# A fused top-k attention and MLP kernel: six MLP chunks of 128 tokens instead of two, no hurried units, kept units further back

## The chip, the cores and the metric

The kernel runs on one core of a Trainium2 chip. The metric is device time in microseconds, from the start to the end of one execution; the median of several runs is given. A core has five engines that work side by side: TensorE (PE in the profile; its weight loads are listed apart as PEld), VectorE (DVE), ScalarE (ACT), GpSimd (POOL) and SyncE (SP), which issues the DMAs. Each engine takes its instructions in the order of the program and waits on semaphores for the others. What follows is about when TensorE is kept from working.

## The reference

Attention over 8 batches of 8 heads, 576 tokens and 64 columns a head, in which each query keeps only its 32 highest scores; then an MLP with a leaky ReLU over the 4608 tokens of all batches, 512 columns wide, 2048 hidden.

```python
scores = scale * np.matmul(q, k.transpose(0, 1, 3, 2))
kth = np.partition(scores, -top_k, axis=-1)[..., -top_k:-top_k + 1]
scores = np.where(scores >= kth, scores, -1000000000.0)
scores = scores - np.max(scores, axis=-1, keepdims=True)
attn = np.exp(scores)
attn = attn / (np.sum(attn, axis=-1, keepdims=True) + 1e-09)
attn_out = np.matmul(attn, v)
...
x = attn_out.transpose(0, 2, 1, 3).reshape(B * S, H * D)
h = x @ w_in
out = np.maximum(0.01 * h, h) @ w_out
```

## The kernel before

**Units and steps.** Attention is cut into 144 units. A unit is 128 query rows of a pair of heads (or twice 64 rows, for what is left of 576), so 32 tokens of all eight heads are worth one unit on average: four units make 128 tokens of x ready, eight make 256. The loop at the end of the program walks through steps `s`; in step `s` unit `s` goes through `top_k` on VectorE (L289: maxima of eight, four rounds), unit `s-1` through mask (GpSimd) and exponents (ScalarE), unit `s-2` through normalising and transposing. Even steps issue the scores of the pair of units `s+2` and `s+3` on TensorE (`scores`, L225).

**Transposing.** The weights of a unit must be transposed before they can be multiplied with the values. `transpose` (L332) has ScalarE split the 32-bit words into halves of 16 bits (L339), writes the halves to DRAM (`apart`, L340) and reads them back with a transposing DMA (L344) into `wT`. `transpose_in_haste` (L346) does the same with nine TensorE transposes (L354), and `keep_transposed` copies the result from PSUM (L360). Units in `HASTY` go that way.

**When values are weighed.** `values_at(n)` gives the step and the place in it, in which unit `n` is multiplied with its values (L381). For `n < 14` that is four steps after the odd unit of the pair, in the middle of the step; from then on three steps after, at its end, and one step sooner for the pairs in `HURRIED`. The result is copied by ScalarE into `x` (L395), of which `xpool` has two buffers.

**The MLP.** `CHUNKS` cuts the 4608 tokens; a chunk is put on the list `ready` when all its units have been weighed. `mlp(ch)` is a generator: it issues matmuls and yields their cost in columns. A chunk of 256 tokens computes hidden values with the weights stationary and x moving (L437, `ph`), 256 columns at a time, then leaky ReLU (L443) into `gT`, then the output (L449, `pz`) with 512 columns. The first `EARLY` chunks, of 128 tokens, take `hidden_of_few` (L399): x is stationary and 512 columns of w_in move (L405), ScalarE applies leaky ReLU into `scale` (L410), and TensorE turns the result in groups of four 128 x 128 transposes (`turned`, L421), which ScalarE copies to `gT` (L422). `ph`, `pt` and `pz` take turns in two PSUM buffers with the tag "ml".

**What sets the order.** Nothing is scheduled by the compiler: the loop calls `mlp_steps(budget)` seven times in a step, which advances the generator until the budget in columns is spent. `slot_budget` gives that budget: as long as no more than the early chunks have become ready it is `EARLY_SHARE`, and later the backlog spread over the slots until the next chunk is ready.

```python
after = [at for (at, _), _ in ready_at if at >= s]
until = after[0] if after else s
if len(after) >= len(CHUNKS) - EARLY:
    return EARLY_SHARE
return backlog[0] / ((until + 1 - s) * SLOTS)
```

**Kept units.** In steps 0 to 5, before any MLP work exists, TensorE computes the scores of twelve units ahead of time (`keep_scores`, L276), from inputs loaded by `load_early`; they are written to DRAM and fetched by `fetch_scores` (L287, 576 KB) three steps before the unit's turn. For `a` in `KEPT` these are units a, a+1, a+8 and a+9. The pairs concerned are then left out when scores are issued.

**SP's queue** carries, in program order, the halves of `split`, the transposing DMAs, the fetches of kept scores, the outputs (L459), and the loads of q, k and v (L651, L179).

Of the kernel before, what the change touches and what calls it, by code (L numbers as in the profile page):

```python
# [20 lines left out]
def kernel(  # L21
# [29 lines left out]
    WCH = 1024  # L51
    LEFT = S % P
    assert D == 64 and S == 576 and HP == 4 and B % 2 == 0 and LEFT == 64
    CHUNKS = [128] * 2 + [256] * 17
    assert sum(CHUNKS) == B * S
    CHMAX = max(CHUNKS)
    LOADED, LOADED_V = 5, 5
# [250 lines left out]
    def mask(u, i):  # L308
        if i == 0:
            u.nbias = small.tile([P, 2], F32, name="nbias")  # L310
            u.z = small.tile([P, 2], F32, name="z")
            nc.gpsimd.tensor_scalar(u.nbias, u.tops[:, :, 0, 0], -SCALE, None, ALU.mult)
        pen = work.tile([P, S], F32, name="pen", bufs=1)
        nc.gpsimd.tensor_scalar(pen, u.s[i], u.tops[:, i, ROUNDS - 1, 7:8], MASKED, ALU.is_lt, ALU.mult)  # L314
        nc.gpsimd.tensor_tensor(u.s[i], u.s[i], pen, ALU.add)  # L315
# [30 lines left out]
    def transpose_in_haste(u):  # L346

        both = u.both.rearrange("p i n -> p (i n)")
        u.parts_T = []
        for c0, c1 in ((0, 8), (8, 2 * NKC - 1)):  # L350
            pt = ps_sc.tile([P, 2, 512], F32, name="wide", bufs=2)
            pt = pt.rearrange("p h (c n) -> p (h c) n", n=P)
            for c in range(c0, c1):
                nc.tensor.transpose(pt[:, c - c0, :], both[:, c * P:(c + 1) * P], ident)  # L354
            u.parts_T.append((c0, c1, pt))

    def keep_transposed(u):
        u.wT = work.tile([P, 2 * NKC - 1, P], F32, name="wT", bufs=3)
        for c0, c1, pt in u.parts_T:
            nc.scalar.copy(u.wT[:, c0:c1, :], pt[:, 0:c1 - c0, :])  # L360

    x_of = {}

    def x_at(token):

        c = 0
        while token >= CHUNKS[c]:
            token -= CHUNKS[c]  # L370
            c += 1
        return c, token
# [15 lines left out]
    def keep_values(u, po):  # L388
        n = u.rows
        po = po.rearrange("p (o n) -> p o n", n=n)  # L390
        ch, col = x_at(u.b * S + u.q0)
        if ch not in x_of:
            x_of[ch] = [xpool.tile([P, CHMAX], F32, name=f"x{c}") for c in range(HP)]
        for o, (pi, _, _) in enumerate(u.outs):
            nc.scalar.copy(x_of[ch][pi % HP][:, col:col + n], po[:, o, :])  # L395

    EARLY = 2

    def hidden_of_few(ch, x):  # L399

        g_of = {}
        for j in range(NFC // 4):
            ph = ps_ml.tile([P, 512], F32, name="ph", tag="ml")
            for c in range(HP):
                nc.tensor.matmul(ph, x[c][:, 0:P], w_in[c][:, j * 512:(j + 1) * 512],  # L405
                                 start=(c == 0), stop=(c == HP - 1))
                if c == 1:
                    yield 2 * 512
            g_of[j] = raws.tile([P, 2 * DMODEL], U16, name="scale", bufs=2).bitcast(F32)
            nc.scalar.activation(g_of[j], ph, AF.Prelu, alpha=SLOPE)  # L410
            yield 2 * 512
            if j:
                yield from turned(j - 1, g_of)
        few[ch] = g_of
# [3 lines left out]
    def turned(j, g_of):  # L418
        pt = ps_ml.tile([P, 4, P], F32, name="pt", tag="ml")
        for i in range(4):  # L420
            nc.tensor.transpose(pt[:, i, :], g_of[j][:, i * P:(i + 1) * P], ident)  # L421
        nc.scalar.copy(gT[:, 4 * j:4 * (j + 1), 0:P], pt)  # L422
        yield 2 * P

    def mlp(ch):

        n = CHUNKS[ch]
        t0 = sum(CHUNKS[:ch])
        x = x_of[ch]
        if ch < EARLY:  # L430
            yield from hidden_of_few(ch, x)
        for f0 in range(0, NFC if ch >= EARLY else 0, 2):
            ph = ps_ml.tile([P, 2, CHMAX], F32, name="ph", tag="ml")
            for i in range(2):
                f = f0 + i
                for c in range(HP):
                    nc.tensor.matmul(  # L437
                        ph[:, i, 0:n], w_in[c][:, f * P:(f + 1) * P], x[c][:, 0:n],
                        start=(c == 0), stop=(c == HP - 1),
                    )  # L440
                    if c == 1 or i == 0 and c == HP - 1:
                        yield 2 * max(n, 225)
            nc.scalar.activation(gT[:, f0:f0 + 2, 0:n], ph[:, :, 0:n], AF.Prelu, alpha=SLOPE)  # L443
            yield 2 * max(n, 225)
        for r0 in range(0, n, P):
            m = min(P, n - r0)
            pz = ps_ml.tile([P, 512], F32, name="pz", tag="ml")
            for f in range(NFC):
                nc.tensor.matmul(  # L449
                    pz[0:m, 0:DMODEL], gT[:, f, r0:r0 + m], w_out[f // 4][:, f % 4, :],  # L450
                    start=(f == 0), stop=(f == NFC - 1),
                )
                if f % 2 and f + 1 < NFC:
                    yield 2 * DMODEL
                if f == 7 and ch in few:
                    yield from turned(NFC // 4 - 1, few[ch])
            o_sb = work.tile([P, DMODEL], F32, name="o_sb", bufs=1)
            nc.scalar.copy(o_sb[0:m], pz[0:m, 0:DMODEL])  # L458
            nc.sync.dma_start(out[t0 + r0:t0 + r0 + m, :], o_sb[0:m])  # L459
            yield 2 * DMODEL  # L460

    def mlp_cost(ch):
        n = CHUNKS[ch]
        if ch < EARLY:
            return NFC * DMODEL + NFC // 4 * (HP * 512 + 2 * P)
# [5 lines left out]
    def mlp_steps(budget):  # L471
        owed[0] += budget
        while owed[0] > 0:
            if running[0] is None:
                if not ready:
                    owed[0] = 0.0
                    return
                running[0] = mlp(ready.pop(0))
            cost = next(running[0], None)
            if cost is None:  # L480
                running[0] = None
            else:
                owed[0] -= cost
                backlog[0] -= cost
# [2 lines left out]

    LAG = 3
    HURRY = 20
    HURRIED = (15, 23, 31)  # L490
    HASTY = (14, 15, 23, 31)
    UNHURRIED = 14
    MIDDLE, END = 0, 1

    def values_at(n):

        if n < UNHURRIED:
            return (n | 1) + LAG + 1, MIDDLE
        return (n | 1) + LAG - ((n | 1) in HURRIED), END

    steps = units

    KEPT = (24, 40, 56)
    EARLY_SCORES = {0: 4, 1: 2, 2: 1, 3: 2, 4: 1, 5: 2}

    def unit(n):
# [3 lines left out]
    for n, u in enumerate(steps):  # L510
        ch, _ = x_at(u.b * S + u.q0)
# [11 lines left out]
    def slot_budget(s):  # L523
# [4 lines that stand above are left out]
            return EARLY_SHARE  # L528
        return backlog[0] / ((until + 1 - s) * SLOTS)

    EARLY_SHARE = 500
    SLOTS = 7

    with tc.manual_schedule():
        last = {p: n for n, u in enumerate(steps) for p in u.pairs}

        to_keep = [[steps[n] for n in (a, a + 1, a + 8, a + 9)] for a in KEPT]
        early_units = {u for us in to_keep for u in us}
# [49 lines left out]
        def weights_of(u):  # L588
            reciprocals(u)
            normalize(u, 0)  # L590
            normalize(u, 1)

        def values(*place):
            due = [u for n, u in enumerate(steps) if values_at(n) == place]
            if due:
                po = ps_sc.tile([P, 2, 512], F32, name="wide", bufs=2)[:, 0, 0:2 * P]
                po = po.rearrange("p (u n) -> p u n", u=2)
            else:
                return ()
            for n, u in enumerate(due):  # L600
                weigh_values(u, po[:, n, :])
            return [(u, po[:, n, :]) for n, u in enumerate(due)]

        def keep(weighed, *place):
            for u, po in weighed:
                keep_values(u, po)
            attended(*place)

        for s in range(len(steps) + LAG + 1):
# [9 lines left out]

            at_first = s < HURRY and s - 2 in HURRIED  # L620
            if at_first:
                weights_of(older)
            slot()
            if old:
                mask(old, 0)
                mask(old, 1)
            late = s < HURRY and not {s - 1, s - 2} & set(HURRIED)
            if older and not late and not at_first:
                weights_of(older)
            mlp_steps(budget)  # L630
            weighed = values(s, MIDDLE)
            at_once = s - 2 in HASTY or any(at == (s, MIDDLE) for at, _ in ready_at)
            if at_once:
                keep(weighed, s, MIDDLE)
            slot()
            if older and late:
                weights_of(older)
            if s - 2 in HASTY:
                transpose_in_haste(older)
# [4 lines left out]
            if older:  # L644
                keep_transposed(older) if s - 2 in HASTY else transpose(older, lambda: mlp_steps(budget))
            if not older or s - 2 in HASTY:
                mlp_steps(budget)
# [83 lines left out]
```

## Time and profile before

| | us |
|---|---|
| median of 3 runs | 1463.28 (1463.24 to 1466.4) |
| the profiled execution | 1463.63 |
| span of the profiled execution | 1461.7 |
| first MLP matmul on TensorE | 130.79 |
| values of units 30 and 31 begin | 372.62 |
| last values begin | 1400.19 |
| MLP of the last chunk begins | 1402.52 |

The granted TensorE clock was 0.985 of full speed over the span. Three forms of rows are used below. A line of groups gives line, engine, operation, output and input, and the busy time. A line of a timeline gives start, duration, engine, line of the kernel, operation, and in brackets the idle time ahead of it with what ended it. A line of the chain of waits gives start, duration and the work that stood on the path that ended last.

Four more groups tell what ScalarE and TensorE do for the small chunks and the hasty units:

```profile
L354 PE MATMUL wide<-ident,s_sb 128*128 128x128 f32 x36 | 5.5, 283 | 0.0
L421 PE MATMUL pt<-ident,scale 128*128 128x128 f32 x32 | 5.0, 278 | 0.0
L410 ACT ACTIVATE scale<-ph 128x512 f32<-128x512 f32 x8 | 4.7, 592 | 1.6 <-PE ph L405 1.6
L422 ACT COPY gT<-pt 128x512 f32<-128x512 f32 x8 | 4.7, 590 | 2.1 <-PE pt L421 2.1
```

### The profile page before, as it was taken

Reading aid. Unit: us, or ns where it says so; the run is one execution under the profiler, and the core shown is the slowest. Engines: PE = TensorE matmul, PEld = TensorE weight load, DVE = VectorE, ACT = ScalarE, POOL = GpSimd, SP = SyncE. Lnnn points to the kernel's source line nnn. Section 1 sums busy time; section 2 is a strip of 40 time slices with the busy share of each in tenths; the row PEclk is TensorE's granted clock in tenths of the full one; section 3 lists DMA queues with packets and bytes.
Section 4 is the critical chain, followed back from the end, with each engine's and each line's share of the span. In section 5 each row is a group of like instructions: output and inputs, shape, how many; then the busy total and the mean of one; then the engine's idle time right before and its main releaser. Section 6 shows DMA issues by size and latency. Waiting matters only on the chain.

```text
span 1461.7 us, 24213 instructions
## 1 busy us (share of the span) xinstructions
PE 1405.5 (96%) x8066; PEld 932.9 (64%) x8068; DVE 1320.3 (90%) x3401; ACT 1100.9 (75%) x1984; POOL 1097.8 (75%) x744
## 2 busy tenths in 40 slices
PE   7848999999989999999999999999999999999998
PEld 2425548576757676767676767676766666666674
DVE  7999999999999999999999999999999999999600
ACT  8878878677868777777778787777777777777710
POOL 3288888878888888888888787888887878787700
PEclk9968999999999999999999999999999999999999
DMA  8967543646576666676656655666566665554510
GB/s 320 344 219 225 140 119 101 194 128 181 151 192 179 172 167 188 156 194 169 157 163 170 169 138 141 171 164 166 149 156 171 164 151 143 153 141 130 150 43 14
DMA packets 394989, 239.03 MB, mean 164 GB/s; under 512 B 334576, under 2 KB 336112, under 8 KB 392944
## 3 DMA queue, kind: packets, MB, share of 16 engines
q1 hardware_dynamic: 394864, 237.48, 58.5%
q8 instruction: 63, 1.03, 0.3%
q14 instruction: 62, 0.51, 0.1%
HBM read 55.77 MB, written 99.09 MB: 106 GB/s over the span
## 4 chain that ended last, share of the span: by engine, by line
PE 77%; DVE 13%; ACT 4%; DMA 4%; issue 1%; SPq 0%; POOL 0%; DVEq 0%; ACTq 0%; POOLq 0%
PE pz L449 30%; PE ph L437 29%; PE wide L381 10%; DVE tops L301 5%; PE wide L225 5%; DVE pairs L304 4%; PE narrow L225 3%; DMA apart<-split 2%; ACT split L339 1%; DVE pairs L296 1%; DMA raw<-in_weights_dram 1%; ACT s_sb L318 1%; ACT s_sb L330 1%; DVE w_out L156 1%; DMA wT<-apart 1%
## 5 line engine op out<-in xcount | busy, mean ns | idle before, releaser
L314 POOL TENSOR_SCALAR pen<-s_sb,tops 128x576 f32<-128x576 f32 x288 | 638.3, 2216 | 203.8 <-DVE tops L301 135.6
L301 DVE MAX8 tops<-pairs 128x8 f32<-128x288 f32 (+1 forms) x1152 | 635.9, 591 | 0.0
L449 PE MATMUL pz<-w_out,gT 128*128 128x512 f32 x1152 | 505.1, 595 | 2.4 <-ACT scale L410 2.4
L437 PE MATMUL ph<-x,w_in 128*128 128x256 f32 x2176 | 482.6, 381 | 0.0
L304 DVE MATCH_REPLACE8 pairs<-tops,pairs 128x288 f32<-128x288 f32 (+1 forms) x864 | 460.1, 538 | 0.0
L437 PEld LDWEIGHTS ph<-x,w_in 128*128 128x128 f32 x2176 | 409.5, 190 | 75.5 <-issue 21.3
L315 POOL TENSOR_TENSOR s_sb<-s_sb,pen 128x576 f32<-128x576 f32 x288 | 406.9, 1413 | 24.0
L449 PEld LDWEIGHTS pz<-w_out,gT 128*128 128x128 f32 x1152 | 216.4, 190 | 266.2 <-issue 261.2
L339 ACT COPY split<-s_sb 128x1152 uint16<-128x1152 uint16 x280 | 309.5, 1146 | 1.7 <-DMA apart<-split 1.7
L330 ACT ACTIVATE s_sb<-s_sb,rz 128x576 f32<-128x576 f32 x288 | 207.7, 773 | 33.4 <-DVE rz L327 33.4
L318 ACT ACTIVATE s_sb<-s_sb,nbias 128x576 f32<-128x576 f32 x288 | 222.4, 772 | 6.4 <-POOL s_sb L315 6.4
L296 DVE TENSOR_TENSOR pairs<-s_sb 128x576 f32<-128x576 f32 x288 | 213.6, 780 | 9.5
L381 PEld LDWEIGHTS wide<-wT,vt 128*64 128x64 f32 x3200 | 161.2, 139 | 53.0 <-issue 36.2
L381 PE MATMUL wide<-wT,vt 128*64 128x128 f32 (+1 forms) x3200 | 179.0, 268 | 10.3 <-DMA wT<-apart 4.7
L443 ACT ACTIVATE gT<-ph 128x512 f32<-128x512 f32 x136 | 80.7, 593 | 58.6 <-PE ph L437 57.7
L395 ACT COPY x<-wide 128x128 f32<-128x128 f32 (+1 forms) x160 | 32.2, 260 | 120.2 <-PE wide L381 120.2
L232 ACT COPY s_sb<-wide 128x704 f32<-128x704 f32 x130 | 98.0, 754 | 20.1 <-PE wide L225 20.1
L458 ACT COPY o_sb<-pz 128x512 f32<-128x512 f32 x36 | 21.1, 585 | 92.3 <-PE pz L449 92.2
L225 PE MATMUL wide<-kt,qt 64*128 64x352 f32 (+1 forms) x360 | 70.4, 507 | 1.0 <-ACT s_sb L247 0.7
L232 ACT COPY s_sb<-narrow 128x448 f32<-128x448 f32 x130 | 62.9, 536 | 1.2 <-PE narrow L225 0.6
L304 DVE MATCH_VALUE_LOAD pairs<-tops,pairs 128x8 f32 x864 | 62.6, 72 | 0.0
L327 DVE RECIPROCAL rz<-ze 128x2 f32<-128x2 f32 x144 | 22.3, 155 | 42.3 <-ACT ze L323 42.1
(67 smaller groups left out, 678.0 us busy)
## 6 DMA issues: line engine op xcount, KB each, us to landing
apart<-split SPq DMA_DIRECT2D x280, 288.0 KB, 2.1
raw<-in_weights_dram SPq DMA_DIRECT2D x15, 1024.0 KB, 6.9
vt<-in_vk_dram SPq DMA_DIRECT2D x32, 320.0 KB, 3.7
out_dram<-o_sb SPq DMA_DIRECT2D x36, 256.0 KB, 2.8
kept<-gT SPq DMA_DIRECT2D x12, 576.0 KB, 3.2
s_sb<-kept SPq DMA_DIRECT2D x12, 576.0 KB, 4.8
qt<-in_qT_dram SPq DMA_DIRECT2D x20, 288.0 KB, 3.5
kt<-in_kT_dram SPq DMA_DIRECT2D x20, 288.0 KB, 3.4
```

The costliest lines, as they stand in the source:

```text
L225: nc.tensor.matmul(to[r0:r0 + u.rows, i, :], qt[d, u.q0:u.q0 + u.rows], kt[d, k0:k1], start=True, stop=True)
L296: nc.vector.tensor_tensor(pairs[:, :, n, :], u.both[:, :, 0:HS], u.both[:, :, HS:S], op)
L301: nc.vector.max(out=u.tops[:, i, r, :], in_=rest[i])
L304: nc.vector.match_replace(out=rest[i], in_to_replace=u.tops[:, i, r, :], in_values=rest[i], imm_value=LOWEST)
L314: nc.gpsimd.tensor_scalar(pen, u.s[i], u.tops[:, i, ROUNDS - 1, 7:8], MASKED, ALU.is_lt, ALU.mult)
L315: nc.gpsimd.tensor_tensor(u.s[i], u.s[i], pen, ALU.add)
L318: nc.scalar.activation(u.s[i], u.s[i], AF.Exp, bias=u.nbias[:, i:i + 1], scale=SCALE, accum_out=u.z[:, i:i + 1])
L330: nc.scalar.activation(u.s[i], u.s[i], AF.Copy, bias=0.0, scale=u.rz[:, i:i + 1])
L339: nc.scalar.copy(split, pairs[:, :, h])
L381: nc.tensor.matmul(po[side * D:(side + 1) * D, o, :], vt[:, c, side, :], u.wT[:, c + side * NKC if c + 1 < NKC else c, r:r + n], start=(c ...
L437: nc.tensor.matmul(ph[:, i, 0:n], w_in[c][:, f * P:(f + 1) * P], x[c][:, 0:n], start=(c == 0), stop=(c == HP - 1),)
L449: nc.tensor.matmul(pz[0:m, 0:DMODEL], gT[:, f, r0:r0 + m], w_out[f // 4][:, f % 4, :], start=(f == 0), stop=(f == NFC - 1),)
```

## The change

The first 768 tokens of the MLP are cut into six chunks of 128 instead of two of 128 and two of 256, and all six take the path of `hidden_of_few`. They become ready in steps 7, 11, 15, 18, 22 and 26; the next chunk, of 256 tokens, in step 34. No unit is hurried or transposed on TensorE any more, so units 14, 15, 23 and 31 take the way through DRAM, and the values of pairs 14/15, 22/23 and 30/31 are weighed one step later than before. The twelve kept units become 72, 73, 80, 81, 96, 97, 104, 105, 112, 113, 120 and 121 instead of 24, 25, 32, 33, 40, 41, 48, 49, 56, 57, 64 and 65. The budget of a slot in the early stage rises from 500 to 550 columns. The set `read` belongs to an assertion made while the program is built, that a buffer of `x` is not taken over before the matmuls that read it have been issued; it adds no instruction.

```diff
-    CHUNKS = [128] * 2 + [256] * 17
+    CHUNKS = [128] * 6 + [256] * 15
...
-    x_of = {}
+    x_of, read = {}, set()
...
         if ch not in x_of:
+            assert ch < 2 or ch - 2 in read
             x_of[ch] = [xpool.tile([P, CHMAX], F32, name=f"x{c}") for c in range(HP)]
...
-    EARLY = 2
+    EARLY = 6
...
         if ch < EARLY:
             yield from hidden_of_few(ch, x)
+            read.add(ch)
...
             yield 2 * max(n, 225)
+        read.add(ch)
         for r0 in range(0, n, P):
...
-    HURRIED = (15, 23, 31)
-    HASTY = (14, 15, 23, 31)
+    HURRIED = ()
+    HASTY = ()
...
-    KEPT = (24, 40, 56)
+    KEPT = (72, 96, 112)
...
-    EARLY_SHARE = 500
+    EARLY_SHARE = 550
```

## The prediction

> **What bounds the kernel now.** I read the page first: the busy shares, the 40 slices, and the chain that ended last by engine.
>
> ```profile
> span 1461.7 us, 24213 instructions
> PE 1405.5 (96%) x8066; PEld 932.9 (64%) x8068; DVE 1320.3 (90%) x3401; ACT 1100.9 (75%) x1984; POOL 1097.8 (75%) x744
> PE   7848999999989999999999999999999999999998
> DVE  7999999999999999999999999999999999999600
> PE 77%; DVE 13%; ACT 4%; DMA 4%; issue 1%; SPq 0%; POOL 0%; DVEq 0%; ACTq 0%; POOLq 0%
> ```
>
> TensorE sets the end over most of the span; VectorE, at 90%, is a close second and ends some 80 us earlier. The average hides two stages, so next I took busy time by stretches of 20 us.
>
> ```profile
> 180.00:200.00 20.00, 16.92 (x105) 8.75 (x104) 19.86 (x56) 16.78 (x32) 17.14 (x12) 0.91 0.45 127
> 420.00:440.00 20.00, 15.75 (x79) 8.82 (x78) 19.93 (x51) 13.22 (x26) 16.19 (x13) 0.91 0.79 209
> 1040.00:1060.00 20.00, 20.00 (x128) 17.02 (x128) 18.15 (x49) 17.13 (x32) 15.44 (x11) 1.00 0.46 126
> ```
>
> Columns: stretch, its length, busy PE, PEld, DVE, ACT, POOL, then granted clock, DMA share, GB/s. Late, TensorE is full and VectorE has gaps; before 440 us there are stretches where VectorE is full and TensorE has holes. Holes on TensorE after its MLP work has begun are what this change can win. Their causes are in TensorE's and ScalarE's timelines, the first such place being:
>
> ```profile
> 186.73 0.60 PE L421 MATMUL pt<-ident,scale 128*128 128x128 f32 x4
> 188.19 3.70 PE L405 MATMUL ph<-w_in,x 128*128 128x512 f32 x8 [0.86 <-ACT scale L410]
> 191.72 0.60 PE L421 MATMUL pt<-ident,scale 128*128 128x128 f32 x4
> 194.47 2.42 PE L449 MATMUL pz<-w_out,gT 128*128 128x512 f32 x4 [2.14 <-ACT scale L410]
> ...
> 191.73 1.44 ACT L330 ACTIVATE s_sb<-s_sb,rz 128x576 f32<-128x576 f32 x2 [1.80 <-DVE rz L327]
> 193.84 0.57 ACT L410 ACTIVATE scale<-ph 128x512 f32<-128x512 f32 x1
> ```
>
> A small chunk's next ph or pz takes the PSUM buffer that ScalarE must first empty (L410), and only 0.5 us of transposes lies between. Here L410 stood behind an L330 that waited for VectorE. The second place is the step in which units 36 and 37 are weighed:
>
> ```profile
> 426.05 1.31 PE L381 MATMUL wide<-wT,vt 128*64 128x128 f32 x20
> 431.61 2.40 PE L381 MATMUL wide<-wT,vt 128*64 128x128 f32 x20 [4.25 <-DMA wT<-apart]
> ...
> 419.74 0.57 SPq L287 DMA_DIRECT2D s_sb<-kept  x1
> ...
> 421.36 5.61 DMA apart<-split
> 427.02 4.55 DMA wT<-apart
> ```
>
> The first two lines are TensorE, the third SP's issues, the last two the chain of waits. A kept unit's 576 KB fetch was issued 1.1 us before unit 37's split halves; those took 5.61 us where the page's median is 2.1, and TensorE stood.
>
> **What the Trainium skill says.** "DMA: Bandwidth & Descriptors", section "Issuing engines are not separate DMA queues": all transfers run on the same 16 engines and interleave. The 5.61 us beside 2.1 agrees. "TensorE: Matmul & The Clock Gate", Part 1: after an idle window of about 3.4 us the array runs at half clock for about as long. The trace agrees: after the 4.25 us hole twenty values matmuls took 2.33 us instead of 1.17 and the scores 2.55 instead of 2.13, so that hole cost 4.4+1.2+0.4, less about 0.2 of ordinary start, 5.8 us. The 2.14 us hole at 192 us was also followed by slow matmuls (0.7 us on pz, 1.2 on scores). The same page, under "Architectural detail", calls ScalarE's queue a strict FIFO; L410 behind L330 is that.
>
> **The change part by part.** Full-speed prices, from starts in TensorE's timeline: ph of 256 columns 0.219 us an instruction (14.01/64), ph or pz of 512 columns 0.429 (13.73/32), a turned group of four transposes 0.49, values of a pair of units 2.33, scores of a pair 2.13, nine hasty transposes 1.26.
>
> Work on TensorE. A 256 chunk is 128 x 0.219 + 64 x 0.429 = 55.5. A 128 chunk is 64 x 0.429 + 4 x 0.49 = 29.4. Four more small for two large: +117.6 - 111.0 = +6.6. The four hasty units give back 4 x 1.26 = 5.0. Net +1.6. The scores kept are twelve units either way, so their sum does not change; only their place does.
>
> ScalarE gains 16 L410 and 16 copies of pt (32 x 0.59 = 19 us), loses 16 L443 (9.5), and trades eight L360 copies (5.1) for eight split copies (9.2): +13 us on an engine 75% busy. SP gains, for those four units, eight split DMAs and four transposing ones; each transfer finds DMA share near 0.55 in those stretches. These sit beside TensorE's work as long as values are not late; if that cover fails, one such delay is priced above, 5.8.
>
> Where the time is won is a question of stages. I compare the moment V when TensorE begins to weigh units 30 and 31: from there MLP chunks, values and pairs are the same in both kernels. Before, V is 372.62, in step 33 (hurried); after, it is in step 34. Up to the first MLP matmul at 130.79 both programs have the same work.
>
> Before, from 130.79: two small chunks 58.8, two large 111.0, 13 pairs of values 30.6 (two of left units are 0.14 dearer), 11 pairs of scores 23.4 (24/25 and 32/33 were kept), hasty 5.0: 228.8. The trace took 241.8. Of the 13.0 over, 5.9 are waits for L410 and their slow matmuls, 1.1 a wait for L360, 2.1 waits of values for vt or wT, and 3.9 small starts.
>
> After: six small chunks 176.4, the same values 30.6, 13 pairs of scores 27.7: 234.7, with 3.9 of small starts V = 369.4 + S, S being waits for L410. In the changed program's order on TensorE a ph or pz follows its transposes with nothing between in 11 places; before in 4 (0.49, 0.36, 0.97 and 4.1 with its slow matmuls). Bounds: 11 x 0.36 = 4.0 and 11 x 1.5 (the mean) = 16.5. I take 0.6 each, the mean of the three ordinary ones: S = 6.6, V = 376.0. The long one needs TensorE to be ahead of VectorE, and here it trails. VectorE allows this: its steps, by starts of L296, are 8.87 us from 142.62 (step 9), so step 35 starts at 373.2 at best; wT of an odd unit in a VectorE-bound stretch lands about 3.5 us before that (431.57 less the 3.5 lost, against step 41's start at 431.57), so V is not under 370. EARLY_SHARE of 550 matches: 7 slots x 550 columns at 1.68 ns are 6.5 us a step, with 2.2 of values and scores 8.7 of 8.87; six chunks of 17,408 columns need 27 steps from step 7, up to step 34. So chunks are neither starved nor left over, and xpool's two buffers are free in time, since a chunk's hidden part is done 2.4 steps after its start.
>
> After V: the start is 376.0 - 372.6 = +3.4. Two more pairs of scores are saved after V (six against four): -4.3. The hole of 5.8 goes, since no fetch stands in steps 37 and 38 and TensorE, without its kept relief there, is again the later engine: -5.8. Chunks and tail are unchanged. Sum -6.7. From the profiled 1463.63: 1456.9; the median of the runs lies 0.35 lower, so 1456.6.
>
> The moved fetches, priced at nothing: an ordinary chunk of eight steps takes 73.79 (670.13 to 743.92), one with a kept pair 71.64 (598.49 to 670.13), and eight VectorE steps 71.0. So TensorE stays the later engine with one pair per chunk, as the new places have it, and in the old ones after 440 us no fetch stopped it. Their bounds are 0 and 5.8 for each couple of fetches.
>
> **The rivals.** *The chain alone.* TensorE's waits hide behind VectorE's pace: V = 370. Then -2.6 - 4.3 - 5.8 = -12.7: 1450.6. For it: in step 34 only 13.5 us of work stand before V, so 4 us of lag would be absorbed. Against it: 11 tight places.
>
> *ScalarE's turnaround.* S = 16.5, V = 385.9: +13.3 - 4.3 - 5.8 = +3.2, 1466.5, no measurable change (I take 0.3%, 4.4 us, as the limit). For it: many of the changed L410 stand right behind an L330, as at 191.7 us, and ScalarE is 13 us fuller. Against: where TensorE trails, rz is long ready.
>
> *Fetches collide late (slower).* In steps 69 to 118 each couple of fetches delays a following split as at 419.74. Price 5.8 a couple; with two of six it is +4.9, with four +16.5 (1479.8); so it decides from two on. For it: values there start only 0 to 2 us after VectorE's next step, so the slack of wT is about 4 us, and a delayed split cost 3.5. Against: old steps 45 to 62 had that slack and held.
>
> That the change doesn't do what it says is ruled out by the order: 96 turned transposes, no hasty ones, twelve fetches at the new places.
>
> **How the numbers follow.** Forecast 0.50 (own range 1454 to 1460), the chain alone 0.20, turnaround 0.20, late fetches 0.10. Range: from the chain's 1450.5 to the turnaround's 1466. Faster: 0.45 + 0.20 + 0.02 = 0.67; within 0.3%: 0.05 + 0.17 = 0.22; slower: 0.01 + 0.10 = 0.11.
>
> **What would show it.** Right: values of units 30/31 start at 374 to 378; 11 or so waits of TensorE for L410, mostly under 1 us; no hole near 430; chunks holding a kept pair at 71.6 and all others at 73.8 us. Wrong: V under 372 or over 380; a hole before L381 between steps 70 and 124; VectorE's steps in 150 to 370 us longer than 8.9; ordinary chunks longer than 74.

## The result, and the profile after

The changed kernel took 1470.26 us in the median of 12 runs (1466.58 to 1474.63), the kernel before 1464.06 (1463.24 to 1466.4). The ratio is 1.0044, with a 95% interval of 1.0033 to 1.0055: 6.4 us slower, where 6.7 us faster was forecast and 1466.0 was the end of the range. The profiled execution took 1469.8 us.

The page of the changed kernel, first parts:

```profile
span 1468.0 us, 24040 instructions
PE 1409.4 (96%) x7968; PEld 912.1 (62%) x7968; DVE 1320.3 (90%) x3401; ACT 1113.3 (76%) x2000; POOL 1097.8 (75%) x744
PE   7848999999999999999999999999999999999999
PE 79%; ACT 7%; DVE 6%; DMA 5%; issue 1%; POOL 1%; SPq 0%; DVEq 0%; POOLq 0%; ACTq 0%
```

ScalarE grew by 12.4 us (13 were worked out), and the 8 in the twelfth of TensorE's slices, the one with the hole near 430 us, has become a 9. But the chain that ended last runs through ScalarE for 7% of the span instead of 4%, and through DMAs for 5% instead of 4%: work was not all that was waited for. The three stretches shown of before, in the changed kernel:

```profile
180.00:200.00 20.00, 18.98 (x95) 10.09 (x96) 19.48 (x50) 17.71 (x33) 16.37 (x11) 1.00 0.59 156
420.00:440.00 20.00, 20.00 (x121) 11.20 (x118) 19.86 (x52) 14.44 (x27) 17.17 (x12) 1.00 0.68 194
1040.00:1060.00 20.00, 20.00 (x123) 15.88 (x121) 19.45 (x51) 15.75 (x29) 15.63 (x13) 1.00 0.61 164
```

The hole near 430 us is filled and the one near 190 us nearly so (18.98 us busy of 20 instead of 16.92), so that much of the change does what was expected. New ones stand elsewhere. TensorE's timeline at the values of units 30/31, and in step 112:

```profile
378.25 1.31 PE L381 MATMUL wide<-wT,vt 128*64 128x128 f32 x20
382.37 2.40 PE L381 MATMUL wide<-wT,vt 128*64 128x128 f32 x20 [2.81 <-DMA wT<-apart]
...
1099.27 1.31 PE L381 MATMUL wide<-wT,vt 128*64 128x128 f32 x20 [2.04 <-DMA wT<-apart]
```

The first costs 2.81 us of idle time and 1.2 us more for twenty matmuls at a reduced clock (2.33 us to the next start instead of 1.17). The second has the same neighbours in SP's queue as the old hole near 430 us:

```profile
1086.95 0.57 SPq L287 DMA_DIRECT2D s_sb<-kept  x1
1087.58 0.42 SPq L179 DMA_DIRECT2D vt<-in_vk_dram  x1
1088.10 0.85 SPq L340 DMA_DIRECT2D apart<-split  x2
```

and the same way of wT in the chain of waits:

```profile
1088.57 5.88 DMA apart<-split
1094.51 4.72 DMA wT<-apart
```

A fetch of kept scores, then v, then at once the split halves of the odd unit whose values are due next. From step 70 on TensorE waits 5.2 us for wT or v, in seven places of more than 0.25 us. Four of them (733, 1025, 1099 and 1171 us; 3.1 us together) are waits for the wT whose halves were issued right behind the fetch of an odd kept unit. A fifth, 1.14 us for v at 937, has the fetch of an even one 0.6 us ahead of the loads of v. The other two (842 and 1356 us) have no fetch near.

The balance of the two profiles, in microseconds after minus before: the first MLP matmul +1.2 (132.02 for 130.79), from there until the values of 30/31 are done +8.5, from there to the end -3.4. The sum is the 6.3 between the spans. Forecast were 0, +3.4 and -10.1. The first is not the change's: over all the profiles shown here the first MLP matmul starts between 130.6 and 132.2 us, with either kind of early chunks.

### The profile page after: what moved, and what is told of

Same layout as the page of the kernel before. It is cut to its first block, busy times and chain, and to the rows that moved or that the text cites. A ratio compares the mean times of both kernels' runs of the same rounds, so it can differ in the third digit from the quotient of the medians.

```text
span 1468.0 us, 24040 instructions
## 1 busy us (share of the span) xinstructions
PE 1409.4 (96%) x7968; PEld 912.1 (62%) x7968; DVE 1320.3 (90%) x3401; ACT 1113.3 (76%) x2000; POOL 1097.8 (75%) x744
## 3 DMA queue, kind: packets, MB, share of 16 engines
q8 instruction: 62, 1.02, 0.3%
## 4 chain that ended last, share of the span: by engine, by line
PE 79%; ACT 7%; DVE 6%; DMA 5%; issue 1%; POOL 1%; SPq 0%; DVEq 0%; POOLq 0%; ACTq 0%
PE pz L452 29%; PE ph L439 27%; PE wide L381 11%; PE wide L225 6%; PE narrow L225 3%; PE ph L406 3%; DMA wT<-apart 3%; ACT split L339 3%; DMA apart<-split 2%; DVE tops L301 2%; ACT s_sb L318 1%; ACT s_sb L330 1%; DVE pairs L304 1%; DVE w_out L156 1%; DVE scale L153 1%
## 5 line engine op out<-in xcount | busy, mean ns | idle before, releaser
L439 PE MATMUL ph<-x,w_in 128*128 128x256 f32 x1920 | 425.6, 381 | 0.0
L439 PEld LDWEIGHTS ph<-x,w_in 128*128 128x128 f32 x1920 | 361.3, 190 | 65.7 <-issue 18.2
L339 ACT COPY split<-s_sb 128x1152 uint16<-128x1152 uint16 x288 | 317.5, 1147 | 0.6 <-DMA apart<-split 0.6
L330 ACT ACTIVATE s_sb<-s_sb,rz 128x576 f32<-128x576 f32 x288 | 207.6, 773 | 36.6 <-DVE rz L327 36.6
L296 DVE TENSOR_TENSOR pairs<-s_sb 128x576 f32<-128x576 f32 x288 | 213.5, 780 | 9.5
L381 PEld LDWEIGHTS wide<-wT,vt 128*64 128x64 f32 x3200 | 162.3, 140 | 56.6 <-issue 35.2
L381 PE MATMUL wide<-wT,vt 128*64 128x128 f32 (+1 forms) x3200 | 181.9, 269 | 12.3 <-DMA wT<-apart 6.9
L445 ACT ACTIVATE gT<-ph 128x512 f32<-128x512 f32 x120 | 71.1, 593 | 63.1 <-PE ph L439 62.6
L406 PE MATMUL ph<-w_in,x 128*128 128x512 f32 x192 | 87.7, 602 | 3.9 <-ACT scale L411 3.9
L327 DVE RECIPROCAL rz<-ze 128x2 f32<-128x2 f32 x144 | 22.3, 155 | 48.2 <-ACT ze L323 47.9
L406 PEld LDWEIGHTS ph<-w_in,x 128*128 128x128 f32 x192 | 35.4, 191 | 46.9 <-issue 39.1
```

The lines of the kernel that those rows point to most:

```text
L296: nc.vector.tensor_tensor(pairs[:, :, n, :], u.both[:, :, 0:HS], u.both[:, :, HS:S], op)
L330: nc.scalar.activation(u.s[i], u.s[i], AF.Copy, bias=0.0, scale=u.rz[:, i:i + 1])
L339: nc.scalar.copy(split, pairs[:, :, h])
L381: nc.tensor.matmul(po[side * D:(side + 1) * D, o, :], vt[:, c, side, :], u.wT[:, c + side * NKC if c + 1 < NKC else c, r:r + n], start=(c ...
L439: nc.tensor.matmul(ph[:, i, 0:n], w_in[c][:, f * P:(f + 1) * P], x[c][:, 0:n], start=(c == 0), stop=(c == HP - 1),)
```

## The experiments

All ratios are against the kernel before, measured in the same series, with 95% intervals. The changed kernel's is 1.0044. Line numbers shift a little between kernels: the leaky ReLU of the small chunks is L410, L411 or L412, the values are L381 or L382. `ze` is the sum of exponents that ScalarE hands to VectorE for its reciprocal (L327); the start of a step is that of VectorE's first L296 in it.

**One part at a time.** Four kernels take one part of the change alone or put one part back.

Kept units moved, nothing else:

```diff
-    KEPT = (24, 40, 56)
+    KEPT = (72, 96, 112)
```

> The kernel before with the kept units moved to 72, 96 and 112 and nothing else. Theory of the holes: the hole near 430 us goes (-5.8 us), but the fetches make new holes of TensorE ahead of values between steps 70 and 124, about 5 us in all as in the changed kernel, so the time is within 3 us of before, and the trace shows these holes. Theory that only TensorE's sum of work counts and the place of the relief is free: -5.8 us, with no new holes.

Measured 1.0010 (1.0003 to 1.0017), 1.5 us slower. The hole near 430 us shrank from 4.25 to 0.50; new ones came at 929.7 (2.61, v), 947.2 (0.70, wT) and 1094.5 (2.66, wT). The free-place theory falls. One thing more: two pairs of scores, 4.3 us of TensorE's work, now stand before the values of units 30/31, and these begin no later. From the first MLP matmul they are 241.9 us away (132.06 to 373.95), before 241.8.

```profile
373.95 2.40 PE L381 MATMUL wide<-wT,vt 128*64 128x128 f32 x40
```

Kept units put back in the changed kernel:

```diff
-    KEPT = (72, 96, 112)
+    KEPT = (24, 40, 56)
```

> The changed kernel with the kept units back at 24, 40 and 56. Theory of the holes: the holes of TensorE after step 70 go (-5.1 us), and two pairs of scores less stand before the values of units 30/31, where TensorE trails, so that these begin 2 to 4 us sooner; the relief after them is 4.3 us smaller. Sum about -3 us against the changed kernel (-7 to +3). Rival, the place of the fetches is innocent and the early stage costs everything: the same as the changed kernel or up to 4 us slower.

Measured 1.0081 (1.0067 to 1.0095), 5.4 us slower than the changed kernel: outside what either theory said. Two readings of its trace bear on this. Its values of 30/31 start at 377.7, against 378.3 with the kept units late, although two pairs of scores (4.3 us of TensorE) fewer stand before them; waits for v and wT (1.87, 0.91 and 0.91 us) have taken their place. So a few microseconds of TensorE's work before that point do not set it. And holes came back near the old fetches, 2.57 us at 438.8 and 2.06 at 586.2; the waits after 390 us come to 7.3 us for the changed kernel's 5.2.

No hurry, nothing else:

```diff
-    HURRIED = (15, 23, 31)
-    HASTY = (14, 15, 23, 31)
+    HURRIED = ()
+    HASTY = ()
```

> The kernel before without hurried or hasty units and nothing else. Theory of the holes: TensorE saves 5.0 us of transposes and a 1.1 us wait, but has no MLP work left between the second small chunk and the first large one, which becomes ready a step (8.9 us) later; its values of units 14/15, 22/23 and 30/31 also wait for wT. +3 to +6 us. Rival, TensorE's work alone counts: -5 to -6 us.

Measured 1.0053 (1.0041 to 1.0066), 7.8 us. The missing MLP work shows as a hole of 2.76 us at 224.3 and one of 8.20 at 233.3: from 215.5 us to 237.0 TensorE has no matmul of the MLP, until the first large chunk is ready. Somewhat dearer than the theory's 3 to 6; the rival falls.

Hurry put back in the changed kernel (the reverse of that edit):

> The changed kernel with the hurried and hasty units of before. If the way of unit 31 through DRAM makes the hole of 4 us at the values of units 30/31, that hole goes and 5.0 us of transposes come: -1 to +3 us. Rival, the missing hurry is what made the change slower: -6 us, back to the time before.

Measured 1.0103 (1.0085 to 1.0122), 8.6 us slower than the changed kernel, where at most 3 was expected. Its values of 30/31 start at 382.0 in step 33, later than the changed kernel's in step 34; TensorE waits for ScalarE's L330 ahead of the hasty transposes (1.52 and 1.35 us). But they are done at 384.4, when the changed kernel's are (384.7), with 1.8 us of small chunks left. VectorE's step 35 begins 4.5 us later (386.8 for 382.4), which is down to 2.0 by step 72 (725.4 for 723.5). Most of the loss comes after that, where the late waits for wT and v have grown: 12.5 us after 390 us instead of 5.2. Why they grow is not shown.

Six chunks and the share of 550, nothing else:

```diff
-    CHUNKS = [128] * 2 + [256] * 17
-    EARLY = 2
-    EARLY_SHARE = 500
+    CHUNKS = [128] * 6 + [256] * 15
+    EARLY = 6
+    EARLY_SHARE = 550
```

> The kernel before with six small chunks and the share of 550, and with its hurried units and kept units as they were. Theory: TensorE's work grows by 6.6 us and it trails VectorE in steps 13 to 33, so that the hurried units' 5 us of transposes buy nothing any more; the moved kept units aside, this is the kernel that came out 15 us slower than before with the hurry put back, so +8 to +14 us. Rival, the parts add up: the changed kernel with old kept places (+11.9 us) less the missing hurry alone (+7.7 us), so +4 us.

Measured 1.0122 (1.0107 to 1.0138), 17.9 us, more than either theory said. Its values of 30/31 begin at 384.4, 11.8 us later than before, and a wait of 6.61 us for wT stands at 448.2. The parts do not add up at all: chunks +17.9 and no hurry +7.8 alone, 11.9 together, 6.4 with the kept units moved as well. Six small chunks need the missing hurry and the late fetches; neither is a gain by itself.

**The fetch.** The fetch of an odd kept unit (in an even step) is put between the split halves and the transposing DMA of its own step. Its buffer is free there, and the transposing DMA waits for the halves anyway.

```diff
-    def transpose(u, between):
+    def transpose(u, between, fetch=lambda: None):
...
             if h == 0:
                 between()
+        fetch()
         u.wT = work.tile([P, 2 * NKC - 1, P], F32, name="wT", bufs=3)
```

> The changed kernel, with the fetch of each odd kept unit issued ahead of the transposing DMA of its step instead of behind it, so that it is through before the next step's split halves. Theory of the fetches: the holes at 733, 1024, 1099 and 1171 us (3.1 us together) go; -2 to -4 us, wT not later elsewhere. Rival, the holes come from VectorE's pace and not from the fetch: they stay, same time.

Measured 0.9999 (0.9991 to 1.0008): about 6 us faster than the changed kernel, more than expected. In the profiles it is 7.5 us, of which 5.1 lie behind the values of units 30/31; the rest lies ahead of the first fetch that was moved, and so is not the edit's. SP's queue around the place shown above:

```profile
1075.35 0.43 SPq L287 DMA_DIRECT2D s_sb<-kept  x1
1080.38 2.56 SPq L345 DMA_TRANSPOSE wT<-apart  x1
...
1083.66 0.85 SPq L340 DMA_DIRECT2D apart<-split  x2
1088.06 2.56 SPq L345 DMA_TRANSPOSE wT<-apart  x1
```

From the halves' issue to the transposing DMA 4.4 us pass instead of 6.4. TensorE's waits after 390 us, first the changed kernel, then this one:

```profile
PE wide L381 <- DMA wT<-apart: 4.1, 6, 2.0
PE wide L381 <- DMA vt<-in_vk_dram: 1.1, 1, 1.1
```

```profile
PE wide L382 <- DMA vt<-in_vk_dram: 1.7, 1, 1.7
PE wide L382 <- DMA wT<-apart: 0.3, 1, 0.3
```

The named waits fall by 3.2 us, and all four of the holes that the theory named are gone; the runs' spread also falls, from 8.1 us (12 runs) to 4.5 (13). The rival, VectorE's pace, falls. What makes up the other 2 us is not shown.

The same edit in the kernel before:

> The same edit in the kernel before. Theory of the fetches: unit 37's halves land in about 2.2 us instead of 5.6, the hole of 4.25 us near 430 us and the slow matmuls behind it go, -3 to -6 us. Rival, VectorE sets the pace there: the hole shrinks but comes back at the next values, -1 to +1 us.

Measured 0.9973 (0.9963 to 0.9984), 4.0 us faster than before. The hole near 430 us is down to 2.38, and the values behind it run at full clock. So the time is as the theory said, though half of the hole stays.

**The early stage.** What makes units 30/31 late was tried from four sides.

The leaky ReLU one slice later in ScalarE's order:

```diff
-            nc.scalar.activation(g_of[j], ph, AF.Prelu, alpha=SLOPE)
             yield 2 * 512
+            nc.scalar.activation(g_of[j], ph, AF.Prelu, alpha=SLOPE)
             if j:
```

> The changed kernel, with the leaky ReLU of a small chunk (L411) put one slice of the budget later in ScalarE's order. Theory of the ring (TensorE trails, ScalarE waits for its ph, and the exponents behind it reach VectorE late): ScalarE's waits for ph fall from 7.8 to under 3 us and VectorE's waits for ze before step 34 from 9.6 to under 6, at the price of longer waits of TensorE for L411 (5.3 us now, 6 to 12 then); sum -3 to +3 us. Rival, the ring does not matter and only TensorE's waits count: +2 to +6 us.

Measured 1.0135 (1.0122 to 1.0149), 13 us slower than the changed kernel. ScalarE's waits for ph fell to 2.4 us as expected, yet VectorE's waits for ze rose from 9.6 to 17.9, and TensorE's for the ReLU to 15.9. The ring as I had drawn it falls: less waiting of ScalarE for ph did not make VectorE any less late.

A lighter share from step 29 on, in the kernel with the odd fetches first:

```diff
-            return EARLY_SHARE
+            return EARLY_SHARE if s < 29 else 450
```

> The changed kernel with the odd fetches first, and the share of a slot lowered from 550 to 450 columns from step 29 on, so that some 7 us of the small chunks' matmuls move from steps 29 to 34 to behind the values of units 30/31. Theory: TensorE trails and drags VectorE in these steps, and then waits for unit 31's wT only because step 34 is light; with the work spread the hole of 2.7 us and the slow matmuls behind it go and the values begin some 3 us sooner net of the work moved, so -3 to -5 us against the kernel with the odd fetches first. Rival, the chain of unit 31 is late by itself: the hole stays or grows, -1 to +4 us.

Measured 0.9998 (0.9990 to 1.0007): no difference. Only 1.7 us of matmuls moved past the values, not 7, since the budget of 550 had some to spare in step 34. The hole is gone, but the values begin at 380.9 instead of 377.1, and waits for ScalarE of 1.02, 1.21 and 1.28 us stand before them. Filling the hole with work shifts the waits.

Half of the hidden matmuls of the small chunks left out, in the kernel with the odd fetches first:

```diff
-            for c in range(HP):
+            for c in range(HP // 2):
...
-                                 start=(c == 0), stop=(c == HP - 1))
+                                 start=(c == 0), stop=(c == HP // 2 - 1))
```

> The changed kernel with the odd fetches first, and with half of the hidden matmuls of the small chunks left out (only the first two of the four blocks of x), which takes 6.9 us a chunk, 41 us in all, from TensorE before the values of units 30/31 and changes nothing on ScalarE, VectorE or in the order. Theory, TensorE is what drags the early steps: VectorE's waits for ze before step 34 fall from 7.2 to under 2 us, its step 35 starts at 372 to 375 instead of 382, and the kernel gets 6 to 9 us faster than the one with the odd fetches first. Rival, ScalarE's fuller queue sets the early pace: VectorE's waits stay at 5 us or more and the time falls by under 3 us.

Measured 0.9998 (0.9988 to 1.0008). With 41 us of TensorE's work gone (at the prices of full clock) the time is the same as with it. TensorE's waits from 140 to 390 us:

```profile
PE ph L407 <- ACT scale L412: 13.3, 6, 3.5
PE pz L453 <- ACT scale L412: 6.8, 4, 2.4
PE wide L382 <- DMA wT<-apart: 4.7, 3, 2.7
PE pt L423 <- ACT scale L412: 3.9, 3, 1.7
```

and its timeline at the values of 30/31:

```profile
374.00 1.31 PE L382 MATMUL wide<-wT,vt 128*64 128x128 f32 x20
377.99 2.19 PE L382 MATMUL wide<-wT,vt 128*64 128x128 f32 x20 [2.68 <-DMA wT<-apart]
```

TensorE spent most of the time saved waiting for ScalarE, and unit 31's wT still arrived only at 378.0, with VectorE's step 35 at 377.7. With all the matmuls these are 381.1 and 381.2. So VectorE's waits for ze (4.9 us for 7.2) and step 35 came out between the two theories, and the 3 us won there were lost again: 1.2 are left at step 41 (433.6 for 434.8), none at the end. TensorE's sum of work does not set the pace of the early stage, although in the changed kernel it is busy for 229.7 of the 235 us from 140 to 375. That it has no part in the pace is not shown, for the emptier TensorE also ran at a lower clock. The two stretches from 140 to 375 us, with all the matmuls and with half:

```profile
140.00:375.00 235.00, 229.96 (x1295) 123.49 (x1294) 226.00 (x590) 196.10 (x366) 190.15 (x127) 1.00 0.56 153
140.00:375.00 235.00, 206.89 (x1227) 112.39 (x1228) 228.28 (x597) 196.29 (x368) 193.62 (x129) 0.94 0.56 153
```

Scores, for which the others wait, were slower in part of it (at 380 us the first group of them took 1.54 us for 0.86), and ScalarE's waits for the wide scores rose from 3.9 to 8.4 us.

Half of ScalarE's work for the small chunks left out instead:

```diff
-            nc.scalar.activation(g_of[j], ph, AF.Prelu, alpha=SLOPE)
+            nc.scalar.activation(g_of[j][:, 0:2 * P], ph[:, 0:2 * P], AF.Prelu, alpha=SLOPE)
...
-        nc.scalar.copy(gT[:, 4 * j:4 * (j + 1), 0:P], pt)
+        nc.scalar.copy(gT[:, 4 * j:4 * j + 2, 0:P], pt[:, 0:2, :])
```

> The same kernel with all its matmuls, but ScalarE does the leaky ReLU and the copy of turned values of the small chunks for half of the columns only, the transposes and output matmuls reading the computed half twice; that takes some 12 us from ScalarE and nothing from TensorE. Theory, TensorE drags: TensorE's waits for L411 fall from 5.3 to 2 or 3 us, time -1 to -4 us, VectorE's waits for ze still 4 us or more. Rival, ScalarE's queue sets the early pace: VectorE's waits fall under 2 us, step 35 starts before 376, -5 to -8 us.

Measured 0.9983 (0.9975 to 0.9991), about 2.3 us faster than with all of it; the two intervals just touch. ScalarE's busy time fell by 9.6 us (1113.0 to 1103.4), not 12. TensorE's waits in the same stretch, first the changed kernel, then this one:

```profile
PE ph L406 <- ACT scale L411: 3.9, 7, 1.2
PE wide L381 <- DMA wT<-apart: 2.8, 1, 2.8
PE pz L452 <- ACT scale L411: 1.4, 4, 0.7
```

```profile
PE wide L382 <- DMA wT<-apart: 2.5, 2, 2.2
PE ph L407 <- ACT scale L412: 1.5, 2, 0.8
PE pz L453 <- ACT scale L412: 0.3, 1, 0.3
```

TensorE's waits for the ReLU fell by 3.5 us, but the wait for wT stays, ending at 377.0. The marks of the theory that TensorE drags are met here, which the half matmuls had not met: neither theory fits both runs. 9.6 us of ScalarE's work were worth some 2.3 us of time. In both kernels VectorE still waits 4.8 or 4.9 us for ze:

```profile
DVE rz L327 <- ACT ze L323: 4.9, 5, 3.2
DVE rz L327 <- ACT ze L323: 4.8, 5, 1.4
```

From step 9 to step 35 VectorE takes 235.9 us in both, 238.3 with all the work, and would take 230.6 at 8.87 us a step. So the way of unit 31 (VectorE, GpSimd, ScalarE, two DMAs) reaches its end at 377 to 378 whichever of the two engines is relieved.

**A faster version.** The kernel before with the kept units moved and the odd fetches first, with its two small chunks and its hurry:

> The kernel before with the kept units moved and the odd fetches first. Theory: the hole near 430 us is gone by the move and the late holes by the order of the fetch, so 3 to 6 us faster than before, like the kernel before with the odd fetches first or better. Rival, the late holes of that kernel come from the loads of v and of kept units together and not from the odd fetch: 0 to +2 us against before.

Measured 0.9953 (0.9941 to 0.9966), median 1459.32 against 1466.33: faster than both, and a little more than expected. Values of 30/31 begin at 372.0, 0.28 us is left of the hole near 430 us, and behind it four waits: 2.21 us for v at 926.9, and 0.47, 0.74 and 0.98 for wT at 998.7, 1071.3 and 1089.6. The one of 2.66 us for wT is gone; the one for v, 2.61 us with the fetches in their old order, stays, so that for this one the rival, v and kept units together, fits. Against the changed kernel with the same fetches (0.9999) this puts 6.7 us on the six chunks without hurry.

## Why the prediction was wrong, point by point

Between the 6.7 us forecast as a gain and the 6.3 us lost in the profiles lie 13.0 us: 1.2 by which the MLP began later, 5.1 from there until the values of units 30/31 were done, 6.7 behind them. Two steps failed.

**The step that failed first: the values of units 30/31 as a sum of TensorE's work, with "VectorE allows this".** "After: six small chunks ... V = 369.4 + S", 376.0, was hit within 2.3 us (378.25; 1.2 of it a later start of the whole stage), and S was 5.3 us for 6.6 said. But the hit is in part luck: V does not follow that sum. 4.3 us more of TensorE's work in the kernel before did not move it (241.9 us from the first MLP matmul for 241.8), 4.3 less in the changed kernel moved it by 0.6, and without 41 us of that work the second half still began at 377.99. The place where the text had the right mechanism was "V is not under 370", which was mis-sized: it let VectorE run at 8.87 us a step and put wT 3.5 us ahead of step 35, at 373.2 at best. VectorE's waits for ze from 140 to 375 us and the start of its step 35, first before, then in the changed kernel:

```profile
DVE rz L327 <- ACT ze L323: 4.1, 4, 2.7
377.37 1.51 DVE L296 TENSOR_TENSOR pairs<-s_sb 128x576 f32<-128x576 f32 x2
DVE rz L327 <- ACT ze L323: 9.6, 8, 2.7
382.36 1.52 DVE L296 TENSOR_TENSOR pairs<-s_sb 128x576 f32<-128x576 f32 x2
```

Already before, VectorE took 9.03 us a step from step 9 to 35, and began that step 4 us later than the best case; this the prediction did not read. In the changed kernel it was some 9 us later, and wT landed at 382.3, level with it. The floor measured 377 to 378 with either engine relieved and 381 to 382 with all the work. From that come the hole of 2.81 us and its 1.2 us of slow matmuls, which the sum did not have; they are 4.0 of the 5.1 us.

**The step that failed second: "the moved fetches, priced at nothing".** They cost about 6 us: that is what putting the odd fetch elsewhere gave back (5.1 in the profiles; the time behind the values of units 30/31 then fell by 8.5 us, of 10.1 forecast). The evidence used, that the old fetches after 440 us stopped nothing, held for one profile of one kernel. The rival of late fetches had the place, the mechanism and the sign right, and its upper count, four of the six couples; its price of 5.8 us a couple was too high (0.26 to 2.04 us of waits, 3.1 together).

**Right.** The hole near 430 us went (0.50 us with the kept units moved alone). The late relief came: TensorE's time from values 30/31 to the end fell by 3.4 us net of the new holes. Waits of TensorE for L410's successor came in 11 places, the largest 1.21 us. ScalarE's 13 us more were 12.4. That the hurry's transposes could go was right, but for another reason than their 5.0 us of TensorE: with them the changed kernel takes 8.6 us more, most of it lost to late waits. A sign named for being wrong came up too: holes before L381 between steps 70 and 124.

**Overtaken.** Where the change was costed on TensorE's sum, +6.6 and -5.0, neither term is what the early stage followed. The same goes for the two pairs of scores that were formerly saved there, 4.3 us that the sum counted as a price of moving them.

**Open.** What sets 377 to 378 is not pinned on one engine. Relieving ScalarE of 9.6 us gave 2.3, relieving TensorE of 41 gave 3 us there and nothing at the end, at a lower clock, and the two were not relieved together. How the 6.7 us that six chunks without hurry cost, the odd fetches first, split between them and the later step of unit 31 is not shown. The share of 550 was never tried apart from the six chunks.

## What to carry to other kernels

An engine that is busy 98% of a stage need not set its pace: where engines wait for each other in order, take half of an engine's work away and see whether the end moves, and look at the clock before you conclude. Here, a prefetch issued just ahead of a short transfer that is due soon was not free, although the DMA engines had room on average (a share of 0.61 in the stretch shown); put it behind the short one and ahead of an instruction that has to wait anyway. A piece of work done early is worth something only if the stage it is taken from is bound by that engine: 4.3 us more of scores ahead of the values of units 30/31 did not delay them here.

## What the runs showed of the hardware that was not expected

TensorE's clock can drop after shorter holes than I had assumed. The clock (the last figure but two) by stretches of 2 us around the hole in the changed kernel:

```profile
378.00:380.00 2.00, 1.56 (x21) 1.07 (x20) 2.00 (x5) 1.78 (x5) 1.92 (x2) 1.00 0.37 81
380.00:382.00 2.00, 0.00 (x0) 0.00 (x0) 2.00 (x5) 2.00 (x3) 0.88 (x3) 1.00 1.23 292
382.00:384.00 2.00, 1.63 (x16) 1.63 (x18) 1.97 (x4) 0.77 (x3) 2.00 (x1) 0.56 0.93 356
384.00:386.00 2.00, 2.00 (x14) 1.31 (x12) 2.00 (x9) 0.43 (x2) 1.82 (x3) 0.58 0.09 21
```

2.81 us idle were enough for a mean granted clock of 0.56 and 0.58 in the next two stretches, and 2.14 us near 194 us in the kernel before for 0.50. The Trainium skill, "TensorE: Matmul & The Clock Gate", Part 1, gives an idle window of about 3.4 us; the measurement decides. But it does not always happen. The same place in the changed kernel with the odd fetches first:

```profile
381.11 1.31 PE L382 MATMUL wide<-wT,vt 128*64 128x128 f32 x20 [2.69 <-DMA wT<-apart]
```

Here 2.69 us idle left the clock at 1.00, and twenty values took 1.31 us for 2.40; the hole of 2.04 us at 1099 us did no harm to it either. What decides between them is not shown by these runs. A hole of 2 to 3 us on TensorE can thus cost 1.2 us more than its length.

The kernels with colliding fetches also seem to scatter more: 1466.6 to 1474.6 for the changed kernel (12 runs), 1463.5 to 1471.4 with only the kept units moved (21), but 1461.7 to 1466.2 (13) and 1458.8 to 1461.2 (5 only) for these two with the fetch in its new place.
